# Weights in their own seats, mask table, seven float32 score blocks, values by four steps, two load queues

## The chip, the cores and the metric

The kernel runs on one core of one Trainium2 chip. The metric is the time of one execution on the device in microseconds (us). Three runs of the kernel before gave a median of 946.76 us (946.31 to 947.65).

## The reference

Inputs: q, k and v of 4 batches x 8 heads x 576 positions x 64, and two pairs of weight matrices (512 x 2048 and 2048 x 512), all float32.

```python
scores = q @ k^T / 8 - 2^-(h+1) * |i - j|     # only where 0 <= i - j < 128, else -1e9
attn   = exp(scores - max);  attn /= attn.sum + 1e-9
x      = (attn @ v), heads side by side         # 2304 tokens x 512
x      = relu(x @ w_in) ** 2 @ w_out            # layer 0
h      = x @ w_in2;  out = (h * cos(h)) @ w_out2   # layer 1
```

## The kernel before

**Tiles.** The 2304 tokens are 18 blocks j of 128. One attention step a = 4j + hp is one block and one pair of heads: 72 steps. A step has scores (L324 or L335), mask and minimum on VectorE (L367), exp on ScalarE (L377), the normalisation (L389, L390, L393), transposes on TensorE (L402), their copy to SBUF on ScalarE (L404) and the values matmuls (L419). Block j sees itself and block j-1. The batch is 576 positions long, so block 4 and block 13 straddle two batches: there mask and exp run in two row halves with different columns (64 rows x 256 and 64 rows x 64).

**Two kinds of scores.** For the first PLAIN = 4 blocks q and k come in as float32 and are multiplied as float32 (L324). For the later ones a "kq" job loads the pair and splits it into a float32r head and a remainder (L277, L278 on ScalarE; L282, L283 on VectorE; L264 and L265 for a block whose k alone is wanted), and the scores are float32r matmuls (L335).

**The two layers.** A unit of ORDER is a token tile b of 512 tokens and a slice f of 128 of the 2048 hidden columns: 12 h matmuls (L463 to L465), the activation, 12 y matmuls (L524 to L526), all float32r with heads and remainders. There are 64 units of layer 0 with 8 more of two slices for the last, half tile, and the same for layer 1.

**Weights.** They arrive as float64 bytes in two halves of 512 values per slice: 64 "w" jobs. A job loads into one of three raw buffers (L164), zeroes a scratch tile on GpSimd (L168), rebuilds float32 with ScalarE (L175) and VectorE (L179), and splits into head (L192, ScalarE) and remainder (L196, VectorE), which live in seats wh0 to wh15 and wl0 to wl15. In the start some seats hold q, k and the exp results of the first steps.

**Order.** The first START = 16 steps run alone. Then unit i runs with the steps that a table of marks asks for (about one step per unit): scores of the next step, h of unit i+1, relu (L469), transposes, squares (L476 to L481), y of unit i, then the values of one or two steps (two as a rule, each by itself where a unit takes two steps). At each tick every job in flight does one stage and at most one job of each kind starts; the loads are issued by SyncE's queue (SP), in the order in which buffers come free. The instructions of an engine run in a fixed order that a scheduler chose beforehand, near the order of the program.

Of the kernel before, what the change touches and what calls it, by code (L numbers as in the profile page):

```python
# [22 lines left out]
P = 128  # L23
NJ = NT // P
# [13 lines left out]

NBK = NB // 2
ORDER = [(0, b, (f,)) for b in range(NBK - 1) for f in range(NF)]  # L40
JOINT = len(ORDER)
for u in range(NU):
    ORDER += [(0, NBK - 1, (2 * u,)), (0, NBK - 1, (2 * u + 1,)), (0, NBK, (2 * u, 2 * u + 1))]
NG1 = len(ORDER)
ORDER += [(1, b, (f,)) for b in range(NBK) for f in range(NF)]
ORDER += [(1, NBK, (2 * u, 2 * u + 1)) for u in range(NU)]
INDEX = {unit: i for i, unit in enumerate(ORDER)}
# [4 lines left out]
START, LOOK, PLAIN = 16, 2, 4  # L52


A_OPEN, W_OPEN, START_W, W1_FROM = 8, 1, 2, JOINT - 2
# [4 lines left out]
class Job:  # L60


    def __init__(self, key, load, stages, gates=None, source=None, frees=1):
        self.key, self.load, self.stages, self.frees = key, load, stages, frees
        self.gates, self.source = gates or {}, source
        self.raw, self.at = None, 0
# [3 lines left out]
def attention_mlp_mlp(ctx: ExitStack, tc: tile.TileContext, kq, k0, q0, v, w1, w2, bias, ident, out):  # L70
# [12 lines left out]
    rp = ctx.enter_context(tc.tile_pool(name="rp", bufs=3))  # L83
# [12 lines left out]
    WH, WL, A2, Y = {}, {}, {}, {}  # L96
    QH, QL, V = {}, {}, {}
    now = {"qk": -1, "h": -1, "y": -1}
# [5 lines left out]
    RAWS = {"a": 2, "w": 3}  # L104
# [4 lines left out]
    def top_up():  # L109
        for c in "aw":  # L110
            if now["qk"] < {"a": A_OPEN, "w": W_OPEN}[c]:
                continue
            jobs = queues[c]
            while held[c] < RAWS[c] and loads[c] < len(jobs):
                job = jobs[loads[c]]
                if job.source is not None and job.source not in finished:
                    break
                job.queue = c
                job.raw = rp.tile([P, 512 if c == "a" else 1024], F32, tag=c, bufs=RAWS[c], name=f"raw_{c}{loads[c]}")
                job.load(job.raw)  # L120
                held[c] += 1
                loads[c] += 1
# [38 lines left out]
    def load_f64(raw, row, half):  # L161


        sp.dma_start(raw.bitcast(U16)[:, 0:2047], row[:, half * 2048 + 1 : half * 2048 + 2048])  # L164

    def f64_zero(job):
        job.t = cv.tile([P, 512], F32, tag="cv", name="cv_" + "_".join(map(str, job.key)))
        pool.memset(job.t, 0.0)  # L168

    def f64_top(job):  # L170
# [6 lines left out]
    def f64_rest(job):  # L177
# [10 lines left out]
    def w_hi(layer, f, half, src):  # L188
        if half == 0:
            WH[layer, f] = wp.tile([P, 1024], F32R, tag=f"wh{f}", name=f"wh_{layer}_{f}")  # L190
            WL[layer, f] = wp.tile([P, 1024], F32R, tag=f"wl{f}", name=f"wl_{layer}_{f}")
        act.copy(WH[layer, f][:, half * 512 : half * 512 + 512], src)  # L192

    def w_lo(layer, f, half, src):
        hs = slice(half * 512, half * 512 + 512)
        dve.tensor_tensor(WL[layer, f][:, hs], src, WH[layer, f][:, hs].bitcast(F32), ALU.subtract)  # L196

    def w_job(layer, f, half):

# [27 lines left out]
    def x2_job(b, m):  # L227
# [7 lines left out]
        def lo(job):  # L235
# [5 lines left out]
            lambda raw: sp.dma_start(raw, y1[b][m]),  # L241
# [9 lines left out]
    def kq_job(j, hp):  # L251
# [7 lines left out]
        if j < PLAIN:  # L259
            return Job(  # L260
                ("kq", j, hp),
                lambda raw: sp.dma_start(raw[:, 0:256], kq[j][:, 512 * hp : 512 * hp + 256]),
# [8 lines left out]
                ],  # L271
            )
# [7 lines left out]
        def lo(job):  # L280
# [6 lines left out]
            lambda raw: sp.dma_start(raw, kq[j][:, 512 * hp : 512 * hp + 512]),  # L287
# [10 lines left out]
    def load_v(j):  # L298
        if j < NJ:
            V[j] = vp.tile([P, H * D], F32, tag="v", name=f"v_{j}")  # L300
            sp.dma_start(V[j], v[j])

    P0 = {}
# [5 lines left out]
    def scores(a):  # L309
# [6 lines left out]
        now["qk"] = a  # L316
        if a < START:
# [3 lines left out]
        if j < PLAIN:  # L321
            for e in range(2):
                for b in (j,) if kind(j) == "first" else (j, j - 1):
                    te.matmul(  # L324
                        sbank[:, e, slot(b) * P : slot(b) * P + P],
                        Q0[j][:, hp, e, :],
                        K0[b][:, hp, :],
# [15 lines left out]
        if a < START:  # L343
            if a % 2 == 0:
                P0[0] = wp.tile([P, 2, 2, 256], F32, tag=f"wh{10 + a // 2 % 4}", name=f"p_{a}")
            pt = P0[0][:, a % 2]
# [3 lines left out]
        Pt[a], St[a] = pt, st  # L350
        b0 = 0 if slot(j) else 128
        kd = kind(j)
        parts = {
            "plain": [(0, 128, 0, 256)],
            "first": [(0, 128, 0, 128)],
            "after": [(0, 128, 64, 256)],
            "straddle": [(0, 64, 0, 256), (64, 128, 64, 128)],
        }[kd]
        if kd == "after":
            pool.memset(pt[:, :, 0:64], 0.0)  # L360
        if kd == "straddle":
            pool.memset(pt[64:128, :, 0:64], 0.0)
            pool.memset(pt[64:128, :, 128:256], 0.0)
        for e in range(2):
            h = 2 * hp + e
            for p0, p1, c0, c1 in parts:
                dve.tensor_tensor_reduce(  # L367
                    out=sbank[p0:p1, e, c0:c1],
                    in0=sbank[p0:p1, e, c0:c1],
                    in1=bias_sb[p0:p1, h, b0 + c0 : b0 + c1],  # L370
                    scale=-0.125,
                    scalar=3.0e38,
                    op0=ALU.add,
                    op1=ALU.min,
                    accum_out=st[p0:p1, e : e + 1],
                )
                act.activation(  # L377
                    pt[p0:p1, e, c0:c1],
                    sbank[p0:p1, e, c0:c1],
                    AF.Exp,  # L380
                    bias=st[p0:p1, e : e + 1],
                    scale=-1.0,
                    accum_out=st[p0:p1, 2 + e : 3 + e],
                )

    def normalise(a):
# [4 lines left out]
        c0, c1 = {"first": (0, 128), "after": (64, 256)}.get(kind(j), (0, 256))  # L391
# [3 lines left out]
    def transposes(s):  # L395
# [9 lines left out]
        Tt[s] = ptT  # L405

    def values(s):
        j, hp = divmod(s, 4)
# [36 lines left out]
    def h_mms(i):  # L445
        layer, b, fs = ORDER[i]
# [3 lines left out]
        for f in fs:  # L450
            run_until(("w", layer, f, 0))
# [4 lines left out]
        for c, f in enumerate(fs):  # L456
            wh, wl = WH[layer, f], WL[layer, f]
            o = hb[:, c] if len(fs) == 2 else hb
            for kt in range(KT):
                cs = slice(kt * P, kt * P + P)  # L460
                xs = XS[x_slot(layer, b)]
                xh, xl = (part[:, 0, kt] if len(fs) == 2 else part[:, :, kt] for part in xs)
# [43 lines left out]
    def y_mms(i, cs, ms=range(KT)):  # L506
        layer, b, fs = ORDER[i]
        run_until(("w", layer, fs[cs[-1]], 1))
        opens, closes = fs[0] == 0, fs[-1] == NF - 1
        per = len(fs)  # L510
        if opens and cs[0] == 0:
            ypool, tag = (ps_y2, "z") if (layer, b) == (0, NBK) else (ps_y, "y")
            Y[b] = [ypool.tile([P, 2, T], F32, tag=f"{tag}{k}", name=f"y_{i}_{k}") for k in range(KT // per)]
        rh, rl = A2[i]
        for m in ms:
            cols = slice(512 + m * P, 512 + m * P + P)
            o = Y[b][m // per]
            if per == 2:
                o = o[:, m % 2]
            for c in cs:  # L520
                wh, wl = WH[layer, fs[c]][:, cols], WL[layer, fs[c]][:, cols]
                gh, gl = (rh[:, c], rl[:, c]) if per == 2 else (rh, rl)
                first, last = opens and c == 0, closes and c == per - 1
                te.matmul(o, wh, gh, start=(first and m % per == 0), stop=False, skip_group_check=True)  # L524
# [47 lines left out]
    start_steps = START  # L572
    LA = 1

    pieces = [(f, half) for f in range(NF) for half in range(2)]
# [3 lines left out]
    queues["w"] += [w_job(layer, *p) for layer in range(2) for p in pieces]  # L579

    with ExitStack():
# [4 lines left out]
        pp = actx.enter_context(tc.tile_pool(name="pp", bufs=3))  # L586
# [6 lines left out]


        Q0, K0 = [], []
        for j in range(PLAIN):
            Q0.append(wp.tile([P, 4, 2, P], F32, tag=f"wl{12 + j}", name=f"q0_{j}"))
            if j % 2 == 0:
                pair = wp.tile([P, 2, 4, P], F32, tag=f"wh{14 + j // 2}", name=f"k0_{j}")
            K0.append(pair[:, j % 2])  # L600
            pool.memset(Q0[j][64:128, :, 0, :], 0.0)
            pool.memset(Q0[j][0:64, :, 1, :], 0.0)
        dve.memset(halfpi, math.pi / 2)

        def load_plain(j):
            sp.dma_start(K0[j].rearrange("p a t -> p (a t)"), k0[j])
            for e in range(2):
                rows = slice(64 * e, 64 * e + 64)
                sp.dma_start(Q0[j][rows, :, e, :], q0[j][rows].rearrange("p (a t) -> p a t", a=4))

# [136 lines left out]
```

## Time and profile before

| | |
|---|---|
| median of 3 runs | 946.76 us |
| profiled execution, its own time | 946.06 us |
| its span, first to last instruction | 944.3 us |
| TensorE matmul busy | 921.9 us (98%) |
| VectorE busy | 599.4 us (63%) |
| ScalarE busy | 522.9 us (55%) |
| GpSimd busy | 43.3 us (5%) |
| mean granted TensorE clock | 0.996 |

Matmuls are pipelined and their ends are modelled, so the busy time of TensorE is not its work: what a matmul takes in a full stream is the distance from one start to the next. In the chain of waits 88% of the span is TensorE, 4% ScalarE, 4% VectorE, 3% DMA.

### The profile page before, as it was taken

How to read it: one execution, taken by the hardware profiler on the slowest of the kernel's cores; microseconds unless marked ns; L12 is line 12 of the kernel's file. 1: busy time of each engine (PE TensorE's matmuls, PEld its weight loads, DVE VectorE, ACT ScalarE, POOL GpSimd, SP SyncE). 2: the span in 40 equal slices, each digit the busy share in tenths (PEclk: the TensorE clock that was granted, in tenths of full speed). 3: DMA queues.
4: the chain of work that ended last, by engine and by line, in shares of the span. 5: the costliest groups of instructions: out<-in, count | busy, mean ns of one | idle time of the engine just before them, and what ended most of it. 6: DMA issues, size and time to landing. Idle time of an engine off the chain costs nothing.

```text
span 944.3 us, 13513 instructions
## 1 busy us (share of the span) xinstructions
PE 921.9 (98%) x4992; PEld 768.4 (81%) x4992; DVE 599.4 (63%) x1403; ACT 522.9 (55%) x1134; POOL 43.3 (5%) x100
## 2 busy tenths in 40 slices
PE   7789999999999999999999999999999999999998
PEld 6567777778787888878888888888888888888898
DVE  4988896666657655555655686566556555655564
ACT  4988885554556645455545574454445444444443
POOL 2011110000000000000101100000000000000000
PEclk9999999999999999999999999999999999999999
DMA  7545663320112111123342440011001000100010
GB/s 215 190 168 190 213 219 98 108 68 34 56 57 101 45 38 53 46 85 116 121 147 89 158 155 1 1 45 45 1 1 40 5 1 1 45 1 1 1 45 23
DMA packets 33954, 71.44 MB, mean 76 GB/s; under 512 B 3424, under 2 KB 10976, under 8 KB 33888
## 3 DMA queue, kind: packets, MB, share of 16 engines
q1 hardware_dynamic: 33888, 70.58, 22.6%
q8 instruction: 39, 0.64, 0.3%
q14 instruction: 27, 0.22, 0.1%
HBM read 61.13 MB, written 9.44 MB: 75 GB/s over the span
## 4 chain that ended last, share of the span: by engine, by line
PE 88%; ACT 4%; DVE 4%; DMA 3%; issue 1%; SPq 0%; POOL 0%; ACTq 0%; DVEq 0%
PE h L464 13%; PE h L463 13%; PE h L465 13%; PE y L524 13%; PE y L525 13%; PE y L526 13%; PE s L335 3%; PE o L419 3%; PE t L402 2%; DMA raw_a<-kq_in 2%; ACT p L377 1%; PE s L324 1%; DVE s L367 1%; ACT cv_w L175 1%; DVE cv_w L179 1%
## 5 line engine op out<-in xcount | busy, mean ns | idle before, releaser
L463 PE MATMUL h<-xh,wh 128*128 128x512 f32 (+1 forms) x640 | 237.3, 371 | 0.6 <-ACT xh L433 0.4
L464 PE MATMUL h<-xl,wh 128*128 128x512 f32 (+1 forms) x640 | 236.8, 370 | 0.3 <-DVE xl L434 0.3
L465 PE MATMUL h<-xh,wl 128*128 128x512 f32 (+1 forms) x640 | 236.3, 369 | 0.0
L463 PEld LDWEIGHTS h<-xh,wh 128*128 128x128 f32 x640 | 121.2, 189 | 20.2 <-ACT a L469 0.7
L465 PEld LDWEIGHTS h<-xh,wl 128*128 128x128 f32 x640 | 121.1, 189 | 20.3
L464 PEld LDWEIGHTS h<-xl,wh 128*128 128x128 f32 x640 | 121.1, 189 | 19.0 <-DVE xl L434 0.7
L524 PE MATMUL y<-rh,wh 128*128 128x512 f32 (+1 forms) x320 | 122.5, 383 | 0.8 <-DVE ysb L539 0.8
L525 PE MATMUL y<-rl,wh 128*128 128x512 f32 (+1 forms) x320 | 118.5, 370 | 0.0
L526 PE MATMUL y<-rh,wl 128*128 128x512 f32 (+1 forms) x320 | 118.4, 370 | 0.0
L524 PE MATMUL y<-gh,wh 128*128 128x512 f32 (+1 forms) x320 | 117.8, 368 | 0.0
L525 PE MATMUL y<-gl,wh 128*128 128x512 f32 (+1 forms) x320 | 117.7, 368 | 0.0
L526 PE MATMUL y<-gh,wl 128*128 128x512 f32 (+1 forms) x320 | 117.7, 368 | 0.0
L492 ACT ACTIVATE r<-r 128x512 f32<-128x512 f32 x72 | 45.4, 631 | 120.0 <-DVE r L491 120.0
L377 ACT ACTIVATE p<-s,st 128x256 f32<-128x256 f32 (+4 forms) x160 | 70.6, 443 | 49.3 <-DVE st L367 47.3
L503 DVE TENSOR_TENSOR gl<-r,gh 128x512 fp32r<-128x512 f32 x72 | 49.8, 691 | 75.1 <-ACT gh L502 75.0
L367 DVE CUSTOM_DVE_ANT_0 s<-s,bias_sb 128x256 f32<-128x256 f32 (+4 forms) x160 | 62.1, 392 | 55.5 <-PE s L335 27.1
L489 DVE SCALAR_TENSOR_TENSOR r<-kk,h 128x512 f32<-128x512 int32 x72 | 49.4, 687 | 68.0 <-ACT kk L488 68.0
L488 ACT ACTIVATE kk<-h 128x512 int32<-128x512 f32 x72 | 43.0, 597 | 75.6 <-PE h L465 75.5
L480 DVE TENSOR_TENSOR a<-a 128x512 f32<-128x512 f32 x62 | 42.8, 691 | 49.0 <-ACT rh L479 46.8
L469 ACT ACTIVATE a<-h 128x512 f32<-128x512 f32 x72 | 42.9, 596 | 51.4 <-PE h L465 50.4
L526 PEld LDWEIGHTS y<-rh,wl 128*128 128x128 f32 x320 | 60.3, 188 | 10.5
L524 PEld LDWEIGHTS y<-rh,wh 128*128 128x128 f32 x320 | 60.4, 189 | 9.9 <-DVE ysb L539 1.3
(60 smaller groups left out, 1389.3 us busy)
## 6 DMA issues: line engine op xcount, KB each, us to landing
raw_w<-w_in SPq DMA_DIRECT2D x64, 511.8 KB, 4.6
raw_a<-kq_in SPq DMA_DIRECT2D x56, 256.0 KB, 2.6
v<-v_in SPq DMA_DIRECT2D x18, 256.0 KB, 3.4
y<-ysb SPq DMA_DIRECT2D x18, 256.0 KB, 2.0
raw_a<-y SPq DMA_DIRECT2D x18, 256.0 KB, 2.7
out<-ysb SPq DMA_DIRECT2D x16, 256.0 KB, 2.5
k<-k_in SPq DMA_DIRECT2D x4, 256.0 KB, 5.5
q<-q_in SPq DMA_DIRECT2D x8, 128.0 KB, 5.6
```

Of the source, the lines that this page charges most:

```text
L367: dve.tensor_tensor_reduce(out=sbank[p0:p1, e, c0:c1], in0=sbank[p0:p1, e, c0:c1], in1=bias_sb[p0:p1, h, b0 + c0 : b0 + c1], scale=-0.125, ...
L377: act.activation(pt[p0:p1, e, c0:c1], sbank[p0:p1, e, c0:c1], AF.Exp, bias=st[p0:p1, e : e + 1], scale=-1.0, accum_out=st[p0:p1, 2 + e : 3 ...
L463: te.matmul(o, wh[:, cs], xh, start=(c == 0 and kt == 0), stop=False, skip_group_check=True)
L464: te.matmul(o, wh[:, cs], xl, start=False, stop=False, skip_group_check=True)
L465: te.matmul(o, wl[:, cs], xh, start=False, stop=(kt == KT - 1), skip_group_check=True)
L488: act.activation(kk, hb, AF.Copy, scale=INV2PI)
L489: dve.scalar_tensor_tensor(r, kk, -C1, hb, ALU.mult, ALU.add)
L492: act.activation(r, r, AF.Abs)
L503: dve.tensor_tensor(rl, r, rh.bitcast(F32), ALU.subtract)
L524: te.matmul(o, wh, gh, start=(first and m % per == 0), stop=False, skip_group_check=True)
L525: te.matmul(o, wh, gl, start=False, stop=False, skip_group_check=True)
L526: te.matmul(o, wl, gh, start=False, stop=last, skip_group_check=True)
```

## The change

- A slice's float64 bytes are loaded whole (1024 values) into the seat w{f}, 8 KB per partition, in which its head and remainder then lie. The raw buffers go; at most two slices are in work at a time. A job has three stages (scratch and ScalarE's part, VectorE's part, split), each on 1024 columns: 32 jobs in place of 64.
- q and k of the first 7 blocks come as float32 (PLAIN = 7), in seats w9 to w15, and so do the exp results of the first 16 steps. Slices 9 to 15 of layer 0 are loaded when the score blocks in their seats are done, slices of layer 1 when layer 0 is done with that slice.
- The straddling blocks take a mask table of their own, and are treated in one piece.
- Values are multiplied for four steps at once (a whole block), between the halves of a unit's y matmuls or after them. Exp tiles: 5 in place of 3.
- At the start mask, identity and the first v are issued by ScalarE's queue, and q and k of the first pair of heads are loaded first.
- The first kq load is allowed from step 20 in place of 8.

```diff
-START, LOOK, PLAIN = 16, 2, 4
-A_OPEN, W_OPEN, START_W, W1_FROM = 8, 1, 2, JOINT - 2
+START, LOOK, PLAIN = 16, 2, 7
+A_OPEN, W_OPEN, START_W = 20, 1, 2
+SEAT = NF - PLAIN
...
-    RAWS = {"a": 2, "w": 3}
+    AHEAD = {"a": 2, "w": 2}
...
+    def w_load(layer, f):
+        def load(job):
+            job.raw = wp.tile([P, 2048], F32, tag=f"w{f}", name=f"raw_{layer}_{f}")
+            sp.dma_start(job.raw.bitcast(U16)[:, 0:4095], (w1, w2)[layer][f][:, 1:4096])
...
+        job.t = cv.tile([P, 1024], F32, tag="cv", name="cv_" + "_".join(map(str, job.key)))
         pool.memset(job.t, 0.0)
...
+    def w_split(job):
+        _, layer, f = job.key
+        w = W[layer, f] = wp.tile([P, 2048], F32R, tag=f"w{f}", name=f"w_{layer}_{f}")
+        act.copy(w[:, 0:1024], job.t)
+        def lo():
+            dve.tensor_tensor(w[:, 1024:2048], job.t, w[:, 0:1024].bitcast(F32), ALU.subtract)
+        late.append(lo)
+    def w_job(layer, f):
+        last = max((i for i, (a, _, fs, _) in enumerate(ORDER) if a == layer - 1 and f in fs), default=-1)
+        seen = 4 * min(f - SEAT + 1, PLAIN - 1) + 3
+        def ready():
+            if layer == 0 and f >= SEAT:
+                return now["qk"] >= seen and now["v"] >= START - 1
+            return now["y"] >= last
+        return Job(("w", layer, f), w_load(layer, f), [w_top, w_rest, w_split], frees=2, ready=ready)
...
+        t = plain(j)
+        if hps.start == 0:
+            pool.memset(t[64:128, :, 0], 0.0)
+            pool.memset(t[0:64, :, 2], 0.0)
+        for e in range(2):
+            rows = slice(64 * e, 64 * e + 64)
+            sp.dma_start(t[rows, hps, e : e + 2], s0[j][rows, hps])
...
+        if hp == 1:
+            load_plain(j + 2)
+            if j == 2:
+                sp.dma_start(strad_sb, strad)
...
-            for p0, p1, c0, c1 in parts:
-                dve.tensor_tensor_reduce(
+            dve.tensor_tensor_reduce(
...
+                in1=strad_sb[:, h] if kd == "straddle" else bias_sb[:, h, b0 + c0 : b0 + c1],
...
+    def values_of_block():
+        if len(waiting) == 4:
+            for q in waiting:
+                values(q)
+            waiting.clear()
...
-        pp = actx.enter_context(tc.tile_pool(name="pp", bufs=3))
+        pp = actx.enter_context(tc.tile_pool(name="pp", bufs=5))
...
-        load_plain(0)
-        sp.dma_start(bias_sb[:, 0:2], bias[:, 0:2])
-        load_v(0)
-        sp.dma_start(id_sb, ident)
-        load_plain(1)
+        load_plain(0, slice(0, 1))
+        act.dma_start(bias_sb[:, 0:2], bias[:, 0:2])
+        load_plain(0, slice(1, 4))
+        act.dma_start(id_sb, ident)
+        load_v(0, act)
+        act.dma_start(bias_sb[:, 2:4], bias[:, 2:4])
+        act.dma_start(bias_sb[:, 4:8], bias[:, 4:8])
+        load_plain(1)
+        load_v(1, act)
...
-            y_mms(i, (0,))
+            if len(ORDER[i][2]) == 2:
+                halves = ((0,), range(KT)), ((1,), range(KT))
+            else:
+                halves = ((0,), (0, 1)), ((0,), (2, 3))
+            y_mms(i, *halves[0])
             if todo > 0:
-                if s % 2 or todo > 1:
-                    for q in range(vdone[0], s + 1):
-                        values(q)
-                    vdone[0] = s + 1
+                values_of_block()
                 s += 1
-            if len(ORDER[i][2]) == 2:
-                y_mms(i, (1,))
-            for _ in range(todo - 1):
-                scores_to(s + 1)
+            if todo > 1:
                 normalise(s)
                 transposes(s)
-                tick()
-                values(s)
-                vdone[0] = s + 1
+                scores_to(s + 1)
                 s += 1
+            y_mms(i, *halves[1])
+            values_of_block()
```

## Rows read from the trace of the kernel before

**Rows 1.** Windows: length, busy us of PE, PEld, DVE, ACT, POOL; clock, DMA share, GB/s.
```profile
0.00:20.00 20.00, 14.29 (x74) 12.58 (x74) 8.22 (x51) 8.21 (x31) 6.53 (x20) 1.00 0.91 252
20.00:52.00 32.00, 24.56 (x204) 18.49 (x202) 29.35 (x113) 28.61 (x82) 2.19 (x4) 0.95 0.48 158
52.00:165.00 113.00, 107.84 (x594) 86.68 (x595) 90.85 (x243) 91.62 (x216) 16.11 (x34) 0.98 0.54 180
...
423.00:944.00 521.00, 518.09 (x2645) 444.06 (x2643) 310.22 (x497) 252.36 (x423) 15.82 (x30) 1.00 0.14 48
```

**Rows 2.** Groups by line, ScalarE, 20 to 52 us: busy, mean ns, idle before.
```profile
L404 ACT COPY p<-t 128x512 f32<-128x512 f32 x12 | 7.1, 588 | 2.0 <-PE t L402 1.8
L175 ACT CAST cv_w<-raw_w 128x512 f16<-128x512 bf16 x6 | 4.7, 777 | 0.0
...
L192 ACT CAST wh<-cv_w 128x512 fp32r<-128x512 f32 x5 | 3.2, 640 | 0.1
L277 ACT CAST KS<-raw_a 128x256 fp32r<-128x256 f32 x5 | 2.0, 399 | 1.2 <-DMA raw_a<-kq_in 1.2
...
L264 ACT CAST KS<-raw_a 128x256 fp32r<-128x256 f32 x4 | 1.6, 403 | 0.1
L278 ACT CAST qh<-raw_a 128x256 fp32r<-128x256 f32 x3 | 1.2, 402 | 0.3 <-PE s L335 0.3
...
L377 ACT ACTIVATION_READ_ACCUMULATOR p<-s,st 64x1 f32 x3 | 0.6, 188 | 0.0
L377 ACT ACTIVATE p<-s,st 64x64 f32<-64x64 f32 x1 | 0.3, 309 | 0.0
```

**Rows 3.** The same view for VectorE, 20 to 52 us.
```profile
L282 DVE TENSOR_TENSOR KS<-raw_a,KS 64x256 fp32r<-64x256 f32 x5 | 2.1, 421 | 0.4 <-ACT KS L277 0.3
```

**Rows 4.** Timeline of the start: start us, us, instruction, idle before.
```profile
2.51 0.60 SPq L612 DMA_DIRECT2D bias_sb<-bias_in  x1
...
7.01 0.30 DVE L367 CUSTOM_DVE_ANT_0 s<-s,bias_sb 128x128 f32<-128x128 f32 x1 [6.15 <-PE s L324]
```

**Rows 5.** The windows view again, 56 to 60 us.
```profile
56.00:60.00 4.00, 3.75 (x14) 2.76 (x14) 2.74 (x8) 2.04 (x7) 0.53 (x1) 0.71 0.63 222
```

**Rows 6.** Chain of work that ended last: start us, us, what.
```profile
56.79 0.43 PE h L465
...
72.00 1.02 PE o L419 x16
...
161.32 1.02 PE o L419 x16
...
309.59 1.02 PE o L419 x16
...
323.63 1.02 PE o L419 x16
```

**Rows 7.** Timeline of TensorE, with and without values between y and h.
```profile
241.49 0.66 PE L419 MATMUL o<-p,v 128*64 128x128 f32 x8
...
323.24 0.39 PE L526 MATMUL y<-rh,wl 128*128 128x512 f32 x1
323.56 1.09 PE L419 MATMUL o<-p,v 128*64 128x128 f32 x16
...
325.16 0.40 PE L463 MATMUL h<-xh,wh 128*128 128x512 f32 x1
...
330.85 0.39 PE L526 MATMUL y<-rh,wl 128*128 128x512 f32 x1
331.07 0.40 PE L335 MATMUL s<-KS,qh 128*128 128x256 f32 x2
...
331.54 0.40 PE L463 MATMUL h<-xh,wh 128*128 128x512 f32 x1
```

**Rows 8.** Timeline of SyncE's queue in the start.
```profile
11.56 11.91 SPq L164 DMA_DIRECT2D raw_w<-w_in  x4
23.51 0.43 SPq L301 DMA_DIRECT2D v<-v_in  x1
```

**Rows 9.** DMA issues on the page: tile, count, KB each, us to landing.
```profile
raw_w<-w_in SPq DMA_DIRECT2D x64, 511.8 KB, 4.6
```

More of the change, by code (lines that the diff above doesn't have):

```diff
@@ L113, in top_up @@
             jobs = queues[c]
-            while held[c] < RAWS[c] and loads[c] < len(jobs):
+            while held[c] < AHEAD[c] and loads[c] < len(jobs):
                 job = jobs[loads[c]]
-                if job.source is not None and job.source not in finished:
+                if job.source is not None and job.source not in finished or job.ready and not job.ready():
                     break
                 job.queue = c
-                job.raw = rp.tile([P, 512 if c == "a" else 1024], F32, tag=c, bufs=RAWS[c], name=f"raw_{c}{loads[c]}")
-                job.load(job.raw)
+                if c == "a":
+                    job.raw = rp.tile([P, 512], F32, tag=c, name=f"raw_{c}{loads[c]}")
+                job.load(job)
                 held[c] += 1
@@ L296, in kind, with cols, load_v, load_plain @@
         return {0: "first", 4: "straddle", 5: "after"}.get(j % 9, "plain")
-    def load_v(j):
+    def cols(j):
+        return {"first": (0, 128), "after": (64, 256)}.get(kind(j), (0, 256))
+    def load_v(j, queue=sp):
         if j < NJ:
             V[j] = vp.tile([P, H * D], F32, tag="v", name=f"v_{j}")
-            sp.dma_start(V[j], v[j])
-    P0 = {}
+            queue.dma_start(V[j], v[j])
+    def load_plain(j, hps=slice(0, 4)):
+        if j >= PLAIN:
+            return
+        t = plain(j)
[5 more added lines that the diff above has]
+            sp.dma_start(t[rows, hps, e : e + 2], s0[j][rows, hps])
+    S0 = [wp.tile([P, 2048], F32, tag=f"w{SEAT + j}", name=f"s0_{j}") for j in range(PLAIN)]
+    def plain(j):
+        return S0[j][:, 0:1536].rearrange("p (a c t) -> p a c t", a=4, c=3)
     def scores_to(a):
@@ L390, in normalise @@
         dve.reciprocal(st[:, 6:8], st[:, 4:6])
-        c0, c1 = {"first": (0, 128), "after": (64, 256)}.get(kind(j), (0, 256))
+        c0, c1 = cols(j)
         for e in range(2):
@@ L405, in transposes @@
         Tt[s] = ptT
+        waiting.append(s)
+    waiting = []
+    def values_of_block():
[3 more added lines that the diff above has]
+            waiting.clear()
     def values(s):
+        now["v"] = s
         j, hp = divmod(s, 4)
@@ L506, in y_mms @@
     def y_mms(i, cs, ms=range(KT)):
-        layer, b, fs = ORDER[i]
-        run_until(("w", layer, fs[cs[-1]], 1))
-        opens, closes = fs[0] == 0, fs[-1] == NF - 1
+        layer, b, fs, n = ORDER[i]
+        opens, closes = fs[0] == 0 and n != 1, fs[-1] == NF - 1
         per = len(fs)
-        if opens and cs[0] == 0:
+        two = b == NBK
+        if opens and cs[0] == 0 and ms[0] == 0:
             ypool, tag = (ps_y2, "z") if (layer, b) == (0, NBK) else (ps_y, "y")
-            Y[b] = [ypool.tile([P, 2, T], F32, tag=f"{tag}{k}", name=f"y_{i}_{k}") for k in range(KT // per)]
+            Y[b] = [ypool.tile([P, 2, T], F32, tag=f"{tag}{k}", name=f"y_{i}_{k}") for k in range(2 if two else KT)]
         rh, rl = A2[i]
         for m in ms:
[L516 to L519, printed above, removed]
+            o = Y[b][m // 2][:, m % 2] if two else Y[b][m] if n is None else Y[b][m][:, n]
             for c in cs:
-                wh, wl = WH[layer, fs[c]][:, cols], WL[layer, fs[c]][:, cols]
+                wh, wl = (W[layer, fs[c]][:, k + m * P : k + m * P + P] for k in (512, 1536))
                 gh, gl = (rh[:, c], rl[:, c]) if per == 2 else (rh, rl)
                 first, last = opens and c == 0, closes and c == per - 1
-                te.matmul(o, wh, gh, start=(first and m % per == 0), stop=False, skip_group_check=True)
+                te.matmul(o, wh, gh, start=(first and not (two and m % 2)), stop=False, skip_group_check=True)
                 te.matmul(o, wh, gl, start=False, stop=False, skip_group_check=True)
@@ L578, in attention_mlp_mlp @@
     queues["a"] += [x2_job(b, m) for b in range(NBK + 1) for m in range(KT if b < NBK else 2)]
-    queues["w"] += [w_job(layer, *p) for layer in range(2) for p in pieces]
+    queues["w"] += [w_job(layer, f) for layer in range(2) for f in range(NF)]
     with ExitStack():
```

176 lines of the change are left out of this document (64 added, 112 removed).

## The prediction

> **What bounds the kernel now.** I read the windows first, since the page's 98% for TensorE is a mean over very different stages. From 423 us to the end TensorE is busy in 518.09 of 521.00 us [rows 1] and the chain runs along it alone: nothing that this change does on other engines can be seen there as long as no weight comes late. In front of that lies the part that can move. From 0 to 20 us the DMA engines are busy 0.91 of the time, and ScalarE and VectorE only 8.2 us each. From 20 to 52 us (steps 5 to 15 of the start) VectorE has 29.35 and ScalarE 28.61 of 32 us: these two set the pace, TensorE has 24.56. From 52 to 165 us (units 0 to 14) ScalarE has 91.62 of 113 us and TensorE 107.84. Then I read the chain for the pace of the units: a pair of units with two steps takes 323.63 - 309.59 = 14.04 us late in the attention, but from 72.00 to 161.32 us six pairs take 89.32 us, 14.89 each [rows 6]. So these units lose 6 x 0.85 = 5.1 us to ScalarE and VectorE. Where TensorE alone sets the pace, what it spends between streams counts: the timeline around a values group says how much [rows 7].
>
> The sum is made against the profiled execution's own 946.06 us (span 944.3 and 1.8 around it); the median of the runs is 946.76, 0.7 above it, and the forecast carries that 0.7.
>
> **The change part by part.**
>
> *Two queues, first pair of heads first.* The first mask transfer leaves SP's queue at 2.51 us behind the q and k loads, and VectorE's first instruction starts at 7.01 [rows 4]. On ScalarE's queue it can leave 0.5 to 1.8 us sooner. I take -1.0; ends 0 and -2.5 us (if it was the mask alone that was waited for, and everything behind it shifts). The Trainium skill (DMA: Bandwidth & Descriptors, Issuing engines are not separate DMA queues) says that loads started from several engines share the same DMA engines and that only the time to issue them is saved; the DMA share of 0.91 over the first 20 us [rows 1] agrees, and by that rule alone this term would be one issue, -0.6 us [rows 4].
>
> *Start, 20 to 52 us.* The window has 12 kq instructions on ScalarE, 2.0 + 1.6 + 1.2 = 4.8 us [rows 2], with their VectorE partners (0.421 us each [rows 3]). With seven float32 blocks none is wanted here. The weights have six rebuilds and five splits here, 4.7 + 3.2 = 7.9 us. Afterwards two whole slices are converted here. A cast of 512 takes 0.640 us and one of 256 some 0.40 [rows 2], so 512 columns more cost about 0.48: estimates of 1.25 us for a rebuild and 1.12 for a split of 1024, 4.7 us for two of each, 3.2 saved. The first straddling step, one extra exp and its accumulator read, 0.3 + 0.2 us. In all 8.5 us of durations; neighbours overlap (the rows of this window add up to 36.5 us where the engine was busy 28.61 [rows 1]), so 8.5 x 0.78 = 6.6 us of ScalarE's time, and about as much on VectorE, where 12 instructions of 0.42 go and four weight steps get shorter. I take -6.0, near the upper end since both pacemakers are relieved alike; ends 0 (the step's own chain, or the loads, hold the pace of 32 / 12 = 2.7 us per step) and -8. Values by blocks put 32 in place of 16 matmuls behind the last copy before h of unit 0: 16 x 0.054 (below) = +0.9, and 0 if the first three steps go ahead; I take +0.7.
>
> *TensorE's clock.* In 56 to 60 us the granted clock is 0.71 [rows 5], and h matmuls of unit 0 follow one another at 0.43 us [rows 6], where a full stream has 331.07 - 330.85 = 0.22 [rows 7]; that is 1.2 against 2.4 GHz. Before it TensorE was busy 24.56 of 32 us. Nine matmuls at 0.2 us more: with a denser start I take -1.8 us; ends 0 and -2.6 (with the transposes).
>
> *Units 0 to 14.* Per unit ScalarE is busy 91.62 / 113 x 7.44 = 6.0 us. Taken out: weights 2 x (0.777 + 0.640) - (1.25 + 1.12) = 0.46 us in each; a kq pair of 0.8 in the first eight units or so; 1.0 in the three straddling steps that are left. Then ScalarE needs under 5.2 of 7.0 us. I take -3.5 of the 5.1 us lost; ends 0 and -5.1.
>
> *Values by four steps.* From the last y matmul to h's first takes 325.16 - 323.24 = 1.92 us with a group of 16 values matmuls and 331.54 - 330.85 = 0.69 without: 1.23. A matmul more costs (1.09 - 0.66) / 8 = 0.054 us, 16 of them 0.86, so a group costs 0.37 us by itself [rows 7]. From 54 to 423 us the 56 steps make 20 groups of two steps (first at 72.00 [rows 6]) and 16 of one (as at 241.49); now 14 of four. 22 x 0.37 = -8.1. Against it: values used to follow the whole y, 2.8 us after the transposes; now half of it, 1.4. ScalarE's copy takes 0.588 us [rows 2] and stands behind a relu; the cover is just long enough, and a 1.25 us rebuild in front of the copy ends it. I take 14 x 0.2 = +2.8; ends 0 and 14 x 0.59 = +8.2.
>
> *Float32 scores in steps 16 to 27.* Same count of matmuls, but float32 between float32r streams. The nearest price of such a change is the group's 0.37: ends 0 and 12 x 0.37 = +4.4 us. I take a third, +1.5, since some stand beside values or transposes.
>
> *What costs nothing.* Layer 1's weights: 1 MB is an estimated 2 x 4.6 = 9.2 us to landing [rows 9] and 5 us of conversion; the last two seats come free when layer 0 ends, and slice 14 is wanted 14 units later, 14 x 24 x 0.22 = 74 us. Seats 14 and 15 of layer 0 come free with step 27, three units (21 us) before slice 14 is wanted: 9.2 + 5 fits, with 7 us to spare. The wait that this adds stands on SP's queue; v and kq loads are behind it, a block (28 us) and a unit (7 us) ahead of need. The mask table (0.5 MB more) and GpSimd (6.53 busy in 20 us) lie beside all this.
>
> Sum: -1.0 - 6.0 + 0.7 - 1.8 - 3.5 - 8.1 + 2.8 + 1.5 = -15.4. 946.06 - 15.4 + 0.7 = **931 us**; if each gain came in at half, 942.
>
> **The rivals.**
>
> 1. *The start does not get shorter.* Its pace is then that of the loads (0 to 20 us: 252 GB/s at 0.91 busy [rows 1]; with whole slices 2 MB of weights stand in SP's queue ahead of the fourth block's q and k) or of a step's own chain. For it: three engines wait for each other in this stage. Against: 29.35 and 28.61 of 32 us busy. Without -6.0 and -1.8: 939 us.
>
> 2. *Grouped values wait for the copy* at its whole length, 8.2 in place of 2.8: 937 us. For it: the cover halves. Against: from unit 15 on ScalarE has room.
>
> 3. *The weight ring becomes the bound: slower.* Only two slices are in work, and the next load is issued at a split. A slice's turn: landing 9.2, stages 1.25 + 1.4 + 1.12 (VectorE's taken alike), and half a unit of ticks, 3.5: 16.5 us, 8.2 per slice with two in work, against 7.02 per unit that TensorE needs. Over slices 3 to 15 that is 13 x 1.2 = +16; if two loads in flight double each other's landing, (25.7 / 2 - 7.02) x 13 = +76. It decides from 8.3 us a unit, where it eats the rest of the gain. With the units' -3.5 gone as well, 950 us and up; I give 955. Against it: seats 0 to 8 are empty at first, so these loads wait for nothing but SP's order, and SP is not held by ScalarE. That SP keeps its order is seen at 11.56: four weight loads, the fourth waiting for its buffer, and a v load with a free place only behind them, at 23.51 [rows 8].
>
> 4. *Seats shared by q, k, exp results and weights chain the steps together* instead of freeing them, so that the change does not do what it says: a step's score load and another step's exp share a tile. If each of the 12 steps after the first four pays another 2 us, 931 + 24 = 955 us.
>
> **How the numbers follow.** Forecast 0.62, rival 1 0.14, rival 2 0.11, rival 3 0.09, rival 4 0.04. The forecast's own range is 922 to 938. The terms at their better ends (-2.5 - 8 - 2.6 - 5.1 - 8.1) give 920; taking in rivals 1 and 2 and half gains, with some loss in the ring, the range is 920 to 944. About 0.2% (1.9 us) can be told from no change. Rivals 3 and 4 are slower but for a ring that only eats the gain: slower 0.11, same 0.03, faster 0.86.
>
> **What would show it.** Unit 0's h matmuls, which still run at 56.79 us [rows 6], should be over by 50. Pairs of units up to unit 14 should take close to 13.9 us. Values should come as 14 groups of 32 (of some 1.9 us), with waits on L404's copy under 0.3 us each. The granted clock should stay at 1.0 between 40 and 56 us. From the end of attention to the end of the span nothing should change (521 us). Waits of ScalarE on weight loads of several us in units 3 to 15 would be rival 3; a start as long as before with ScalarE and VectorE half idle, rivals 1 or 4.

## The result, and the profile after

The changed kernel takes 936.12 us (median of 4 runs, 934.74 to 938.28), the kernel before 946.53 us on the same chip (4 runs, 945.56 to 947.65): ratio 0.9895, 95% interval 0.9879 to 0.9912. It is 10.4 us faster; 15.4 had been forecast.

The profiled execution of after took 934.74 us, span 933.0, so its span is 11.3 us shorter than that of before. The starts of four instructions in the two timelines of TensorE divide this:

| | before | after | difference of the stretch |
|---|---|---|---|
| first h matmul of unit 0 | 53.94 | 53.52 | -0.4 |
| first y matmul of unit 0 | 62.69 | 60.58 | -1.7 |
| first y matmul of unit 14 | 165.94 | 160.25 | -3.6 |
| end of the span | 944.3 | 933.0 | -5.6 |

The prediction had 8.1 us of gain in front of the first y (-1.0 - 6.0 + 0.7 - 1.8) and 7.3 behind it. Measured are 2.1 and 9.2: the start failed, the rest came out above the forecast. The windows show both (columns as in [rows 1]; here and below a block shows rows picked from a view, and the rows between them are left out):

```profile
core 0: us, PE busy (x) PEld busy (x) DVE busy (x) ACT busy (x) POOL busy (x), PEclk, DMA share, GB/s
0.00:20.00 20.00, 9.73 (x69) 8.74 (x70) 7.74 (x49) 8.55 (x32) 9.25 (x20) 1.00 0.95 255
20.00:52.00 32.00, 24.82 (x212) 20.57 (x211) 27.57 (x98) 26.16 (x65) 3.82 (x4) 0.89 0.75 205
52.00:160.00 108.00, 107.89 (x625) 90.31 (x626) 77.45 (x188) 78.30 (x161) 12.27 (x16) 1.00 0.37 141
160.00:412.00 252.00, 251.64 (x1501) 209.40 (x1500) 160.47 (x487) 141.15 (x368) 0.82 (x4) 1.00 0.19 65
412.00:933.00 521.00, 517.57 (x2638) 443.40 (x2636) 306.96 (x466) 248.68 (x392) 13.40 (x14) 1.00 0.15 52
```

From 20 to 52 us VectorE was relieved by 1.8 us (29.35 to 27.57) and ScalarE by 2.4 (28.61 to 26.16), where the prediction wanted 6.6 from each; both then idle while TensorE does no more than before. From 52 us on TensorE has 0.1 us left to lose in 108. The 521 us behind the attention are what they were.

What filled the start is seen in the groups of ScalarE and VectorE (20 to 50 us; busy us, mean ns of one, idle time before), which answer to [rows 2, 3]. The kq work is gone, but four whole slices are converted here, not two:

```profile
L185 ACT CAST cv_w<-raw 128x1024 f16<-128x1024 bf16 x4 | 5.4, 1358 | 0.0
L201 ACT CAST w<-cv_w 128x1024 fp32r<-128x1024 f32 x4 | 4.2, 1056 | 0.0
L189 DVE SCALAR_TENSOR_TENSOR cv_w<-raw,cv_w 128x1024 int32<-128x1024 int32 x4 | 4.9, 1224 | 0.2
L204 DVE TENSOR_TENSOR w<-cv_w,w 128x1024 fp32r<-128x1024 f32 x4 | 4.9, 1220 | 0.0
```

Slices 0 and 1 start in the first two steps by the program (START_W = 2). Slices 2 and 3 start in the ticks of the first units, behind all 16 steps; the scheduler, which fixes each engine's order beforehand, moved their stages in between the steps. That costs at two places. At the earlier one a mask is done at 24.4 us (L386 on VectorE), but its exp (L396) comes at 26.28, behind a split and a rebuild on ScalarE, and TensorE's next scores wait for that exp (timelines: start, duration, engine, line; in brackets idle time before it and what ended it):

```profile
24.13 1.05 ACT L201 CAST w<-cv_w 128x1024 fp32r<-128x1024 f32 x1
25.08 1.33 ACT L185 CAST cv_w<-raw 128x1024 f16<-128x1024 bf16 x1
26.28 0.47 ACT L396 ACTIVATE s<-s,st 128x256 f32<-128x256 f32 x1
```

```profile
26.89 0.49 PE L354 MATMUL s<-s 128*128 128x128 f32 x2 [1.69 <-ACT s L396]
```

The later one, first on VectorE and then on TensorE:

```profile
41.97 1.22 DVE L204 TENSOR_TENSOR w<-cv_w,w 128x1024 fp32r<-128x1024 f32 x1
43.11 0.68 DVE L464 TENSOR_TENSOR xl<-o,xh 128x512 fp32r<-128x512 f32 x1
43.84 1.22 DVE L204 TENSOR_TENSOR w<-cv_w,w 128x1024 fp32r<-128x1024 f32 x1
44.98 0.42 DVE L386 CUSTOM_DVE_ANT_0 s<-s,bias_sb 128x256 f32<-128x256 f32 x1
45.32 0.22 DVE L409 RECIPROCAL st<-st 128x2 f32<-128x2 f32 x2
45.52 1.54 DVE L412 TENSOR_SCALAR s<-s,st 128x256 f32<-128x256 f32 x4
```

```profile
41.60 0.63 PE L421 MATMUL t<-id_sb,s 128*128 128x128 f32 x4 [0.37 <-DVE s L412]
43.94 1.12 PE L449 MATMUL o<-s,v 128*64 128x128 f32 x8 [1.71 <-DVE xl L464]
46.33 0.69 PE L421 MATMUL t<-id_sb,s 128*128 128x128 f32 x2 [1.27 <-DMA s<-s_in]
46.81 0.64 PE L354 MATMUL s<-s 128*128 128x128 f32 x2
```

The wait at 46.33 is put down to a load, but the normalisation begun at 45.52 is as late. Two splits of weights that nothing wants before 53 us stand ahead of the normalisation of two steps. TensorE stands still behind them from 42.2 to 46.3 us but for 1.1 us, and its clock falls. Windows of 4 us:

```profile
40.00:44.00 4.00, 1.92 (x20) 1.23 (x18) 3.25 (x11) 4.00 (x12) 0.69 (x1) 0.94 0.41 116
44.00:48.00 4.00, 2.73 (x16) 2.33 (x17) 3.92 (x15) 0.66 (x4) 1.21 (x2) 0.50 1.04 247
48.00:52.00 4.00, 3.93 (x30) 3.02 (x29) 0.98 (x4) 2.17 (x6) 0.00 (x0) 0.71 0.23 96
```

TensorE had 1.92 of 4 us, then the granted clock is 0.50 (1.2 GHz) while ScalarE has little to do (0.66 of 4). The reader is to see that all three engines are badly used here: it is an order that binds, no engine.

### The profile page after: what moved, and what is told of

It is laid out like the page before. It is cut to its first block, busy times and chain, and to the rows that moved or that the text cites. A ratio compares the mean times of both kernels' runs of the same rounds, so it can differ in the third digit from the quotient of the medians.

```text
span 933.0 us, 13113 instructions
## 1 busy us (share of the span) xinstructions
PE 911.6 (98%) x5040; PEld 772.4 (83%) x5040; DVE 580.2 (62%) x1283; ACT 502.8 (54%) x1014; POOL 39.6 (4%) x58
## 4 chain that ended last, share of the span: by engine, by line
PE 91%; ACT 4%; DVE 2%; DMA 2%; issue 1%; SPq 0%; POOL 0%; ACTq 0%; DVEq 0%
PE y L552 14%; PE y L554 13%; PE y L553 13%; PE h L493 13%; PE h L494 13%; PE h L495 13%; PE o L449 3%; PE t L421 3%; PE s L365 2%; PE s L354 2%; DMA s<-s_in 1%; ACT cv_w L185 1%; DVE cv_w L189 0%; ACT s L396 0%; ACT w L201 0%
## 5 line engine op out<-in xcount | busy, mean ns | idle before, releaser
L493 PE MATMUL h<-xh,w 128*128 128x512 f32 (+1 forms) x640 | 237.2, 371 | 0.0
L494 PE MATMUL h<-xl,w 128*128 128x512 f32 (+1 forms) x640 | 236.1, 369 | 0.0
L495 PE MATMUL h<-xh,w 128*128 128x512 f32 (+1 forms) x640 | 235.6, 368 | 0.0
L495 PEld LDWEIGHTS h<-xh,w 128*128 128x128 f32 x640 | 120.6, 188 | 20.4
L493 PEld LDWEIGHTS h<-xh,w 128*128 128x128 f32 x640 | 120.8, 189 | 19.4 <-ACT ysb L567 0.2
L494 PEld LDWEIGHTS h<-xl,w 128*128 128x128 f32 x640 | 120.9, 189 | 18.5
L552 PE MATMUL y<-rh,w 128*128 128x512 f32 (+1 forms) x320 | 123.4, 387 | 0.4 <-DVE ysb L567 0.4
L554 PE MATMUL y<-rh,w 128*128 128x512 f32 (+1 forms) x320 | 118.4, 370 | 0.0
L553 PE MATMUL y<-rl,w 128*128 128x512 f32 (+1 forms) x320 | 118.2, 370 | 0.0
L552 PE MATMUL y<-gh,w 128*128 128x512 f32 (+1 forms) x320 | 117.8, 369 | 0.2 <-ACT gh L532 0.2
L553 PE MATMUL y<-gl,w 128*128 128x512 f32 (+1 forms) x320 | 117.7, 368 | 0.0
L554 PE MATMUL y<-gh,w 128*128 128x512 f32 (+1 forms) x320 | 117.7, 368 | 0.0
L396 ACT ACTIVATE p<-s,st 128x256 f32<-128x256 f32 (+2 forms) x112 | 51.5, 460 | 54.5 <-DVE st L386 54.4
L386 DVE CUSTOM_DVE_ANT_0 s<-s,bias_sb 128x256 f32<-128x256 f32 (+2 forms) x128 | 51.5, 407 | 38.6 <-PE s L354 13.9
L554 PEld LDWEIGHTS y<-rh,w 128*128 128x128 f32 x320 | 60.3, 188 | 10.7
L552 PEld LDWEIGHTS y<-rh,w 128*128 128x128 f32 x320 | 60.4, 189 | 10.4 <-issue 1.7
```

What stands on the lines that cost most here:

```text
L386: dve.tensor_tensor_reduce(out=sbank[:, e, c0:c1], in0=sbank[:, e, c0:c1], in1=strad_sb[:, h] if kd == "straddle" else bias_sb[:, h, b0 + ...
L396: act.activation(pt[:, e, c0:c1], sbank[:, e, c0:c1], AF.Exp, bias=st[:, e : e + 1], scale=-1.0, accum_out=st[:, 2 + e : 3 + e],)
L493: te.matmul(o, wh[:, cs], xh, start=(c == 0 and kt == 0), stop=False, skip_group_check=True)
L494: te.matmul(o, wh[:, cs], xl, start=False, stop=False, skip_group_check=True)
L495: te.matmul(o, wl[:, cs], xh, start=False, stop=(kt == KT - 1), skip_group_check=True)
L552: te.matmul(o, wh, gh, start=(first and not (two and m % 2)), stop=False, skip_group_check=True)
```

## The experiments

Ratios are to the kernel before on the same chip. Runs 1 to 4, 5 to 8 and 9 to 12 had one chip for each four. First h is the start of unit 0's first h matmul in the run's profile. Line numbers are those of the run's own kernel.

**1. No conversions in the start.**

```diff
+    def w_zero(job):
+        _, layer, f = job.key
+        w = W[layer, f] = wp.tile([P, 2048], F32R, tag=f"w{f}", name=f"w_{layer}_{f}")
+        pool.memset(w.bitcast(F32), 0.0)
...
-        return Job(..., [w_top, w_rest, w_split], ...)
+        return Job(..., [skip, skip, w_zero] if layer == 0 and f < 4 else [w_top, w_rest, w_split], ...)
```

> The changed kernel, but slices 0 to 3 of layer 0 are loaded and not converted (GpSimd writes zeros to their seats). In the changed kernel these four conversions stand in the start: 9.6 us on ScalarE and as much on VectorE between 20 and 52 us. Theory A, they hold the start at its old length: the first h matmul moves from 53.5 us to 45 to 48, total about 929. Theory B, the loads hold it (DMA engines full from 4 to 32 us): the first h matmul stays within 1.5 us of 53.5, total 935 to 936. Theory C, the chain of a step by itself: also no move beyond 1.5 us, with ScalarE and VectorE idle for a third of the stage.

936.94 us, ratio 0.988 (0.9851 to 0.991); first h at 51.42, 2.1 us sooner than in after, and more than that lost later: unit 14's first y comes at 162.63, after's at 160.25, and 2.4 us of it are one wait for a copy (L431), as in run 6. This test did not isolate what it should: its four zeroings on GpSimd hold up VectorE (the last section), so the conversions' share of the start is only bounded from below, by 2 us. Run 6 repeats it without them.

**2. Values by two steps.**

```diff
-        if len(waiting) == 4:
+        if len(waiting) == 2:
```

> The changed kernel with values by two steps in place of four. Theory A, a group costs 0.37 us by itself: about 13 more groups from 56 to 411 us, +4 to +5 us, 940 to 941, all of it after 56 us. Theory B, the gain of that stage came from ScalarE's relief and not from grouping: 936 within 1.

942.38 us, ratio 0.9943 (0.9923 to 0.9963): about 5 us more than after. In the profile 4.7 us of the difference to after stand behind the first y, where there are 14 more groups: 0.33 us each, near the forecast's 0.37. Another 3.0 us stand in front of it (first h at 55.82), which neither theory had.

**3. Five blocks of float32 scores.**

```diff
-START, LOOK, PLAIN = 16, 2, 7
-A_OPEN, W_OPEN, START_W = 20, 1, 2
+START, LOOK, PLAIN, SEATS = 16, 2, 5, 7
+A_OPEN, W_OPEN, START_W = 12, 1, 2
...
```

> The changed kernel with 5 float32 score blocks in place of 7 (seats as before, kq loads from step 12). Theory A, a float32 score step costs TensorE 0.40 us more than a float32r one where TensorE is the bound: 8 steps, -3.2 us, about 933. Theory B, the kq work that returns (0.8 us on ScalarE per step) makes ScalarE and VectorE the bound in units 2 to 10 again, as before the change: 936 to 939, with gaps of 1 us and more on TensorE there.

937.37 us, ratio 0.9895 (0.9867 to 0.9922). The time is that of after, and the profile shows two effects against each other. One is what a step's scores cost beside a unit. A step has four matmuls in either form. The float32 ones (L354) leave eight records, two for each, the float32r ones (L365) four. TensorE's timelines, of after and of this kernel:

```profile
85.37 0.38 PE L354 MATMUL s<-s 128*128 128x128 f32 x2
85.59 0.39 PE L354 MATMUL s<-s,s 128*128 128x128 f32 x2
85.81 0.39 PE L354 MATMUL s<-s 128*128 128x128 f32 x2
86.04 0.39 PE L354 MATMUL s<-s,s 128*128 128x128 f32 x2
86.18 0.48 PE L493 MATMUL h<-xh,w 128*128 128x512 f32 x1
86.49 0.40 PE L494 MATMUL h<-xl,w 128*128 128x512 f32 x1
```

```profile
93.80 0.40 PE L365 MATMUL s<-KS,qh 128*128 128x256 f32 x2
94.03 0.40 PE L365 MATMUL s<-KS,ql 128*128 128x256 f32 x2
94.27 0.40 PE L493 MATMUL h<-xh,w 128*128 128x512 f32 x1
94.51 0.40 PE L494 MATMUL h<-xl,w 128*128 128x512 f32 x1
```

Two records take 0.22 us in float32, of 128 columns each, and 0.23 to 0.24 in float32r, of 256 each. The float32 stage takes 86.18 - 85.37 = 0.81 us, the other 0.47, and the first h matmul after it 0.31 in place of 0.24. A unit's period is 6.84 with float32 scores (85.37 to 92.21 in the timeline) and 6.43 without (93.80 to 100.23): 0.41 a step. Four pairs at 0.22 are 0.88, and 0.81 and 0.07 add up to it, so all of the 0.41 can be the scores' own work; that the change of form costs anything by itself is not shown. From the first y to unit 14's this kernel needs 97.4 us, after 99.7. The other effect: its first h comes at 59.81; between 20 and 52 us ScalarE rebuilds a fifth slice (L185 x5) and casts keys (L270 x2). In the profiled execution, at 940.47 us the slowest of the four, the loss in the start is the larger one.

**4. All first loads on one queue.**

```diff
-        act.dma_start(bias_sb[:, 0:2], bias[:, 0:2])
+        sp.dma_start(bias_sb[:, 0:2], bias[:, 0:2])
...
-        load_v(0, act)
+        load_v(0)
```

> The changed kernel with all loads of the start on SyncE's queue, in the same order. Theory A, the second queue saves issue time only and the first scores wait for q and k: first exp later by up to 1 us, total +0 to +1. Theory B, the second queue carries the start: +2 us and more. Theory C, it makes mask and v compete with q and k, whose first scores came 0.7 us later than before the change: -0.5 to -1.5.

936.96 us, ratio 0.9883 (0.9856 to 0.9909), the same as after: the second queue is worth nothing that can be measured in the time. In the start it costs first and gains later. With one queue the first scores start at 3.90 us and VectorE's first instruction at 5.13, in after at 5.21 and 6.44, which is theory C's place; but the fourth step's transposes are copied at 20.2, in after at 17.4, and first h comes at 55.57.

**5. After, once more, beside the next three.**

> The changed kernel itself once more, on the chip of the next three runs, so that they can be compared with it: 0.988 to 0.991 of the kernel before. In its trace the first h matmul stands between 52 and 57 us, by how TensorE's clock falls in the start.

936.81 us, ratio 0.9883 (0.9864 to 0.9902). First h at 54.22, and TensorE's waits from 20 to 54 us are those of after to a tenth of a microsecond: the order makes them, not chance.

**6. One slice converted in the start.**

```diff
+    def w_same(job):
+        _, layer, f = job.key
+        W[layer, f] = W[0, 0]
...
+        ... [skip, skip, w_same] if layer == 0 and 0 < f < 4 else [w_top, w_rest, w_split] ...
```

> The changed kernel, but slices 1 to 3 of layer 0 are loaded and not converted; their units use slice 0's seat. Three of the four conversions that stand in the start are gone (7.2 us on ScalarE, 7.3 on VectorE), and unlike in the run without four conversions GpSimd writes no big tile beside VectorE. Theory A, the conversions hold the start: first h 5 to 7 us earlier than in the repeat of the changed kernel, total -5 or more. Theory B, loads or the step's chain hold it: within 2 us.

939.21 us (934.93 to 941.7), ratio 0.9905 (0.987 to 0.994), but the place answers: first h at 50.03, 4.2 us before run 5. The conversions do hold the start: the loads of the four slices leave SyncE's queue by 15.8 us as in run 5 (15.4). In the profiled execution, the slowest of the four, the gain is lost again at two places: TensorE waits 2.4 us at 110 and 2.8 us at 165 us, and behind each its granted clock is 0.50 for 3.4 us. ScalarE's timeline at the first, and what TensorE's weight loads waited for (97 to 112 us: us in total, times, longest):

```profile
105.47 1.36 ACT L192 CAST cv_w<-raw 128x1024 f16<-128x1024 bf16 x1 [1.98 <-DMA raw<-w_in]
108.12 1.05 ACT L208 CAST w<-cv_w 128x1024 fp32r<-128x1024 f32 x1 [1.03 <-DVE cv_w L196]
111.33 0.57 ACT L430 COPY p<-t 128x512 f32<-128x512 f32 x1
```

```profile
PEld o L456 <- ACT p L430: 2.7, 1, 2.7
```

A rebuild whose load left SP at 98.32 and landed at 105.4 and its split stand in ScalarE's order ahead of the copy (L430) that TensorE's values want. The weight ring, rival 3, does bite, at one place, once the start is shorter: 2.7 us and not 24. At the second place a step's normalisation (L419) stands behind the split of a slice whose rebuild waited for no load.

**7. No weight job started inside the 16 steps.**

```diff
-A_OPEN, W_OPEN, START_W = 20, 1, 2
+A_OPEN, W_OPEN, START_W = 20, 1, 0
```

> The changed kernel with no weight job started inside the first 16 steps (START_W 0): the first two slices lose their place ahead of the steps, and their conversions are put where the engines have room. Theory A, it is their place ahead of the steps' own work that costs: first h 2 to 4 us earlier, total -2 to -4. Theory B, the amount of work counts and not its place: within 1 us, or later, when the first slice is then late for h of unit 0.

932.71 us (931.95 to 932.96), ratio 0.984 (0.9823 to 0.9857), below run 5's interval: theory A, a little beyond its range. First h at 49.63, 4.6 us sooner than in run 5. Three slices are still converted before 50 us (L185 and L201 x3), but the steps go first. TensorE's waits from 20 to 54 us, of after and of this kernel:

```profile
PE t L421 <- DVE s L412: 1.7, 2, 1.4
PE o L449 <- DVE xl L464: 1.7, 1, 1.7
PE s L354 <- ACT s L396: 1.7, 1, 1.7
PE t L421 <- DMA s<-s_in: 1.3, 1, 1.3
PE o L449 <- ACT s L423: 0.7, 1, 0.7
```

```profile
PE o L449 <- ACT s L423: 1.3, 2, 0.7
PE o L449 <- DVE st L408: 1.0, 1, 1.0
PE t L421 <- DVE s L412: 0.6, 1, 0.6
```

7.1 us against 2.9: the difference of 4.2 is nearly the whole shift of the first h. And the granted clock, in the same stretch, does not fall (what that alone is worth was not separated):

```profile
44.00:48.00 4.00, 3.32 (x31) 2.14 (x29) 2.78 (x6) 3.25 (x7) 0.00 (x0) 1.00 1.09 320
48.00:52.00 4.00, 3.78 (x25) 3.00 (x26) 3.09 (x12) 2.55 (x7) 0.95 (x1) 1.00 0.65 229
```

By itself this run leaves the loads open as a cause: slices 2 and 3 leave SyncE's queue at 34.4 and 43.0 us here, in after at 10.2 and 14.2. Run 6 closes that, with early loads and the same first h. The two together also part place from amount: with one slice converted first h comes at 50.03, with three at 49.63.

**8. Each conversion stage in two instructions of 512 columns.**

```diff
-        act.copy(w[:, 0:1024], job.t)
+        for c in (slice(0, 512), slice(512, 1024)):
+            act.copy(w[:, c], job.t[:, c])
...
```

> The changed kernel with each conversion stage in two instructions of 512 columns. Theory A, the long instructions save fixed time but block the steps behind them: in the start no loss, in units 0 to 14 nothing, since TensorE is the bound there; total within 1.5 us. Theory B, the 0.4 us saved per unit on ScalarE were needed in units 0 to 14: gaps on TensorE come back, +2 to +4.

935.78 us (933.31 to 936.21), ratio 0.9865 (0.9841 to 0.9889): its interval overlaps run 5's; first h at 52.90. The length of one instruction is not what costs the 4 us.

**9. Run 7's kernel again.**

> The kernel after with START_W = 0 (no weight job started inside the 16 steps), on another chip beside the next three. Theory A (the place of the conversions ahead of the steps is what the start costs): 932.5 us again, ratio 0.984, first h matmul of unit 0 at 49.5 to 51 us. Rival B (its 4 us were the granted clock of one run): 936 us, ratio 0.988, first h at 53 us or later.

931.79 us (931.17 to 933.79), ratio 0.9852 (0.9831 to 0.9874); first h at 48.95, the same three waits in the start. Theory A, on a second chip.

**10. Runs 7 and 8 together.**

> START_W = 0, and each conversion stage in two instructions of 512 columns. Theory A (what a long instruction takes is not the matter, its place in the fixed order is): within 1 us of START_W = 0 alone, 932 to 933.5 us, since the halves add some 0.2 us per instruction on engines with room. Rival B (a step's copy or normalisation waits behind a whole 1024-column cast, 1.36 us, and halves let it through): 931 us or below, and TensorE's waits on ScalarE and VectorE between 56 and 165 us smaller.

932.76 us, ratio 0.9867 (0.9841 to 0.9893): theory A in the time. The first h comes at 46.11, 2.8 us sooner than in run 9, so the halves do let the steps through, but by unit 14 only 1.0 of the lead is left (155.88, run 9: 156.87): TensorE waits 1.4 us for a relu and 1.3 us for a copy between 46 and 160 us, which run 7 does not.

**11. Run 7 with five float32 blocks.** The edits of runs 3 and 7.

> START_W = 0 and five blocks of float32 scores in place of seven (kq jobs from step 12). Theory A (a float32 step costs 0.40 us more between float32r streams, and the start was long in the run with five blocks because conversions stood ahead of its steps): 8 of the 12 float32 steps beside units go, -3.2 us, against the kq work of two steps or so in the start, +1: 930.5 us. Rival B (the kq casts in the start hold it by themselves, as in the earlier run with five blocks, whose first h came 6 us later): 936 us, first h after 55 us.

934.01 us (930.81 to 936.13), ratio 0.9869 (0.9841 to 0.9898). Theory A's number lies outside the interval (930.5 would be 0.983), rival B's inside (936, 0.9885). In the profile both effects are there: first y to unit 14's takes 97.5 us (run 7: 100.8), but the first h comes at 54.19. The order chosen has five rebuilds between 20 and 52 us again (L185 x5), VectorE's normalisations keep TensorE waiting for 3.4 us, and the granted clock is 0.50 from 48 to 52 us. Rival B's place, then, in this execution (934.37).

**12. Run 7 with six.**

```diff
-START, LOOK, PLAIN = 16, 2, 7
-A_OPEN, W_OPEN, START_W = 20, 1, 2
+START, LOOK, PLAIN, SEATS = 16, 2, 6, 7
+A_OPEN, W_OPEN, START_W = 16, 1, 0
```

> START_W = 0 and six blocks of float32 scores (kq jobs from step 16, the first step beside a unit). Theory A: 4 of the 12 float32 steps go, -1.6 us, and almost no kq work lies in the start: 931 us, first h at 50 to 51 us. Rival B (kq jobs beside the first units take as much from ScalarE as the float32 scores from TensorE): 932.5 us or more, with h or scores waiting for ScalarE in units 0 to 6.

932.55 us, ratio 0.9857 (0.9833 to 0.988), the same as run 9, as rival B had it in the time but not in the place. First y to unit 14's takes 97.9 us, 2.9 less than in run 7; the first h comes 1.8 us later than there, the first y follows it 0.8 later than there, and from unit 14 to the end of attention another 0.8 is lost (TensorE waits 1.1 us for a copy of y, 0.4 in run 7). What is saved on float32 scores is lost again; that the casts beside the start take it was not tested. None of runs 10 to 12 is better than START_W = 0 alone on the same chip (run 9, 931.8 us), which is 4 us below the changed kernel.

## Why the prediction was right in sign and 5 us off

*Two queues (-1.0).* VectorE's first instruction starts at 6.44 in place of 7.01 [rows 4]: -0.6, the number that the prediction gave for the case that only the time to issue is saved. That it came out is chance: in run 4, with one queue, it starts at 5.13, so that the new order of the loads gained 1.9 and the second queue took 1.3 of it back. The Trainium skill (DMA: Bandwidth & Descriptors, Issuing engines are not separate DMA queues) states that loads of several issuing engines share the same DMA engines. The times agree, 0.9883 with one queue (run 4) and 0.9883 with two (run 5).

*Start, 20 to 52 us (-6.0): the step that failed.* The prediction said "afterwards two whole slices are converted here". There were four. Its prices of one were near (rebuild 1.25 estimated, 1.36 measured; split 1.12 and 1.06), so its 8.5 us of durations taken off become 8.5 - 2 x (1.36 + 1.06) = 3.7, and by its own factor 0.78 ScalarE is relieved by 2.9; measured 2.4. Even that did not reach the end of the start, where the first h gained 0.4, because of where the other conversions stand (runs 6 and 7). Busy shares of two pacemakers were read as if the work were all on the path; in a fixed order it matters what stands ahead of a step. With START_W = 0 the first h comes 4.3 us (run 7) and 5.0 us (run 9) sooner than before, less than the 6.3 forecast for head, body and tail, and the kernel takes 932, against 931 forecast.

*Rival 1* had the right place and outcome for this stage, 939 us with the clock term lost as well. Its mechanisms were the loads or a step's own chain. Run 6 has the same early loads, run 7 the same work in its steps, and both begin h over 4 us sooner than run 5: neither held the start at its length. What holds it at 49 to 50 us after that is open.

*TensorE's clock (-1.8).* From the first h to the first y it is 8.75 and 7.06 us: -1.7, as forecast, since unit 0's h now runs at full clock. That is luck. The reason given was a denser start, and the start is not denser; the sign given, a granted clock of 1.0 from 40 to 56 us, did not come: it fell to 0.50 earlier, and was back at 1.0 before unit 0 began.

*Units 0 to 14 (-3.5) and float32 scores (+1.5).* Stretch by stretch the two go together: -3.6 to unit 14. The stalls on ScalarE and VectorE are gone altogether: from 56 to 420 us TensorE's largest wait is 0.8 us. So -5.1, the end of the range. The scores cost 12 x 0.41 = +4.9, above the upper end of 4.4. The prediction said "same count of matmuls, but float32 between float32r streams", and priced the change between the streams. No price of that is seen; the same count in float32 is twice the records, 0.41 us more in every step (run 3).

*Values by four steps (-8.1 + 2.8).* A group, in after's timeline:

```profile
111.10 0.40 PE L554 MATMUL y<-rh,w 128*128 128x512 f32 x1
111.42 1.97 PE L449 MATMUL o<-p,v 128*64 128x128 f32 x32
113.32 0.50 PE L552 MATMUL y<-rh,w 128*128 128x512 f32 x1
```

From L554's start to L552's it is 2.22 us, of which 0.23 is the y matmul in its stream; 32 x 0.054 = 1.73 is work, so that a group still costs some 0.3 by itself, and with the slower y matmul behind it (0.34 in place of 0.23) 0.4. So -8.1 is about right (22 groups at run 2's 0.33 are -7.3). The +2.8 for copies did not come: from 56 us on TensorE waits for L423 at values once, 0.3 us. Rival 2 is out.

Behind the first y: -8.1 + 0.3 - 5.1 + 4.9 = -8.0 of the -9.2 measured; 1.2 us stay without a name. By stretch the prices do less well: 4 groups fewer in front of unit 14 and 18 behind it give -1.4 and -6.7, measured are -3.6 and -5.6.

*Rivals 3 and 4.* ScalarE waits for a weight load once in after's units, 0.4 us, though a 1 MB load takes 10.7 us to land in the first 56 us (median of ten), longer than the 9.2 estimated; run 6 shows 2.7 us at one place. One score of the start waits 1.7 us for an exp (L354 behind L396, shown above). Whether a shared seat makes it wait is not shown, and the exp itself stood behind two casts; 12 waits of 2 us would be rival 4, and there is one.

## What to carry to other kernels

Where a fixed order binds, count what the scheduler will move in front of the critical steps, not what the program starts there: letting two prefetch jobs begin in the first steps, and not behind all 16, cost 4 us here, and one number gave it back. Three engines at 0.8 to 0.9 busy and none at 1 was the sign of a chain here; relieving two of them by about 2 us moved nothing. An equal count of matmuls is not equal work where the number format differs: take TensorE's time per step for either form from the trace.

## What was not expected of the hardware

A zeroing on GpSimd stops one kind of VectorE instruction until it ends. Run 1, GpSimd's timeline and VectorE's; L420 is L412 of after:

```profile
25.26 1.97 POOL L184 MEMSET w<- 128x2048 f32 x1 [2.00 <-DMA raw<-w_in]
```

```profile
24.61 0.41 DVE L394 CUSTOM_DVE_ANT_0 s<-s,bias_sb 128x256 f32<-128x256 f32 x1
25.14 2.24 DVE L420 TENSOR_SCALAR s<-s,st 128x256 f32<-128x256 f32 x2
27.30 0.41 DVE L394 CUSTOM_DVE_ANT_0 s<-s,bias_sb 128x256 f32<-128x256 f32 x1
```

The two tensor_scalar instructions, 0.62 us as a rule, take 2.24 and end 0.15 us behind the zeroing (27.23). The run's three other zeroings (at 18.98, 21.46 and 31.91) do the same to L416 at 20.02 (0.80), L420 at 21.63 (1.78) and L416's pair at 31.98 (1.76), which all end within 0.15 us of them; a mask instruction (L394) inside the first takes 0.47. The Trainium skill (SBUF — State Buffer, Who interferes with whom) states that tensor_scalar in a mode that uses two ports shares a pair of them with GpSimd, and that the second to come waits for the whole instruction of the first; the rows agree. In after the scratch zeroings (0.96 us each, L183) do the same on a small scale: L412's pair at 30.64 takes 0.86.

That a float32 matmul leaves two records of 0.11 us for 128 columns, where a float32r one leaves a single record of 0.11 to 0.12 for 256, was not expected either: a float32 step of four matmuls takes 0.81 us to the start of the next one and its float32r form 0.47 (run 3).
